# 128-column zero matmuls, a first weight piece of 384 columns on two queues, and two units moved by one place

## The chip, the cores and the metric

The kernel runs on one core of a Trainium2 chip. Its five engines work from streams of their own and meet through semaphores: TensorE (PE in the profile; its weight loads are listed as PEld), VectorE (DVE), ScalarE (ACT), GpSimd (POOL) and SyncE (SP), which here only issues DMA transfers. ScalarE issues a few transfers too. The metric is the device time of one execution in microseconds (us). The profile also gives the span, from the first to the last instruction of the program.

## The reference

The input `x` is 2048 x 512, bfloat16. Its rows are normalized, and the sum of three terms comes out: `x` itself, a spectral filter of the normalized rows, and a gated feed-forward block on them.

```python
def _A_ref(x, w_r, w_i):
    X = jnp.fft.rfft2(x.astype(jnp.float32), axes=(-2, -1))
    X = X * (w_r + 1j * w_i)
    return jnp.fft.irfft2(X, s=(S, D), axes=(-2, -1)).astype(jnp.bfloat16)

def _B_ref(x, w_gate, w_up, w_down):
    g = jnp.einsum("bsd,df->bsf", x, w_gate)
    u = jnp.einsum("bsd,df->bsf", x, w_up)
    return jnp.einsum("bsf,fd->bsd", _gelu(g) * u, w_down)

xn = _layernorm(x, axis=-1)
return x + _A_ref(xn, A_w_r, A_w_i) + _B_ref(xn, B_w_gate, B_w_up, B_w_down)
```

There are 2048 rows, 512 columns and 1792 features between `w_gate`/`w_up` and `w_down`.

## The kernel before

The 2048 rows are 16 tiles of 128 rows; four tiles make a block of 512 rows. The 1792 features are 14 chunks (`fc`) of 128.

**Normalization** (`ln_stats`, `ln_rstd`, `ln_apply`): VectorE takes mean and variance of a tile (L401, L402). The reciprocal root comes from ScalarE for tiles 0 and 1 (L407) and from GpSimd for all later ones (L416, L417). VectorE applies it (L424). TensorE then transposes the tile (L442, four 128 x 128 pieces a tile, against a unit matrix), and VectorE and ScalarE copy the transposes from the accumulation banks into `xnT` (L449, L451).

**Feed-forward**: `geglu_unit(b, fc)` makes one chunk for one block: four matmuls with `wg_sb` and four with `wu_sb` (L499), the gelu on ScalarE (L511), the product on VectorE into `hT` (L519). The first six chunks of block 0 are done in two halves of 256 rows, so that they can begin when tiles 0 and 1 are there. `down_unit(b, jj)` makes one output tile: 14 matmuls of `hT` with `wd_sb` (L547; the last tile in two halves of 14), and the sum into `x_sb` on VectorE (L553).

**Spectral branch**: GpSimd folds the halves of `xnT` (L463, L464), `unit_d` and `unit_A` transform along columns and rows (L571, L587), the result goes through memory (`shuffle`) into another order, `unit_B` and `unit_c` finish the transform, multiply by the filter and go back (L618 to L645), 64 small transfers reorder again (L650), `unit_e` (L665, copied by ScalarE at L670) and `unit_fin` (L685 to L697) come back to rows and columns and add to `x_sb`.

**Order.** Each engine's stream is the order in which the program records its operations; `emit` puts a semaphore wait before an operation where it depends on another engine. An engine never passes an operation that waits. The order on TensorE is written out by hand from L703 on: the zeros, the normalization of tiles 0 and 1, their transposes, the twelve half chunks with the transposes of tiles 2 and 3 between (after the half chunk `fc` 3), and then the spectral units with *fillers* between them. `filler(n)` takes the next n units from one list of all remaining feed-forward units (`geglu_unit` and `down_unit` of blocks 0 to 3 in a fixed order), so that TensorE has work while a spectral unit waits for its copies. `spare` is the number of fillers spread over the 18 steps of `unit_B` and `unit_c`, worked out so that four are left over for the end.

**Zeros.** `warm_up` (L473 to L483) has TensorE multiply zeros, 18 times with 512 columns, from a memset of `hT[1]`; the results are not used. The memset is the third operation on VectorE's stream.

**Transfers.** SP issues nearly all loads in one order, ScalarE the unit matrix and weight piece 0. `WPIECES` cuts the columns of `w_gate` and `w_up` into four pieces, 256, 512, 512 and 512 wide; each piece is two transfers under one semaphore, and a chunk's first matmul waits for both transfers of each piece that its 128 columns touch. So piece 0 serves chunks 0 and 1, piece 1 chunks 2 to 5, piece 2 chunks 6 to 9, piece 3 the rest. The order before: on ScalarE the unit matrix, `wg` and `wu` of piece 0; on SP x tiles 0 to 3 (one each), piece 1, x tiles 4 to 7, piece 2, x tiles 8 to 15, piece 3, constants, `w_down`.

Of the kernel before, what the change touches and what calls it, by code (L numbers as in the profile page):

```python
# [16 lines left out]
FF = 1792  # L17
P = 128
# [3 lines left out]
NFC = 14  # L22
NGG = 3
NX1 = 4
NWARM = 18
LN_EPS = 1e-5


# [131 lines left out]
class _Sched:  # L160
# [14 lines left out]
    def total(self, stream):  # L175
        return (stream, self.stream_cnt[stream])
# [59 lines left out]
def bass_parallel_sum__spectral_gfnet__glu_gated_geglu__prompt_kernel(  # L236
# [15 lines left out]
    xv = A_x.rearrange("b (p j) d -> p (b j) d", j=NJ)  # L252
# [3 lines left out]
    sch = _Sched()  # L256

    with ExitStack() as es:

        def sb(name, shape, dt=BF16):  # L260
            return es.enter_context(nc.sbuf_tensor(name, shape, dt))

        x_sb = sb("x_sb", [P, NJ, D])
        xnT = sb("xnT", [P, NDC, S])
        wg_sb = sb("wg_sb", [P, NDC, FF])
        wu_sb = sb("wu_sb", [P, NDC, FF])
        wd_sb = sb("wd_sb", [P, NFC, D])
        hT = [sb("hT%d" % i, [P, NFC, 512]) for i in range(2)]
# [45 lines left out]
        def bank_of(slot):  # L314
            return ps[:, slot * 512:(slot + 1) * 512]
# [25 lines left out]
        def load(stream, dst, src, eng="sp"):  # L341
            sch.op(eng, lambda e: e.dma_start(dst, src), stream=stream)
            return total(stream)


        ev_id = load("ident", small[:, 0:P], c_small.ap()[:, 0:P], eng="act")
        ev_x = {}
        for j in range(4):
            ev_x[j] = load("x%d" % j, x_sb[:, j, :], xv[:, j, :])

        WPIECES = ((0, 256), (256, 768), (768, 1280), (1280, FF))
        ev_w = {}
        spec = {}

        def load_w(i, eng="sp"):
            a, b = WPIECES[i]
            for dst, src in ((wg_sb, B_w_gate), (wu_sb, B_w_up)):
                load("w%d" % i, dst[:, :, a:b], src[:, a:b].rearrange("(r p) f -> p r f", p=P), eng=eng)
            ev_w[i] = total("w%d" % i)

        def load_xc(m):
            ev = load("xc%d" % m, x_sb[:, 4 * m:4 * m + 4, :], xv[:, 4 * m:4 * m + 4, :])
            for j in range(4 * m, 4 * m + 4):
                ev_x[j] = ev

        load_w(0, eng="act")
        load_w(1)
        load_xc(1)
        load_w(2)
        load_xc(2)  # L370
        load_xc(3)
# [21 lines left out]
            spec["eg"] = total("eg")  # L393


        ev_eps = sch.op("pool", lambda e: e.memset(eps_t[:], LN_EPS))
        ev_half = sch.op("pool", lambda e: e.memset(half_t[:], -0.5))
        ev_ag = {}
# [61 lines left out]
        def folds(m, after=()):  # L460
            sl = slice(m * 512, (m + 1) * 512)
            deps = [ev_xnT[4 * m], ev_xnT[4 * m + 3]] + list(after)
            a = sch.op("pool", lambda e: e.tensor_tensor(fold[:, 0:2, sl], xnT[:, 0:2, sl], xnT[:, 2:4, sl], ALU.add), deps=deps)  # L463
            b = sch.op("pool", lambda e: e.tensor_tensor(fold[:, 2:4, sl], xnT[:, 0:2, sl], xnT[:, 2:4, sl], ALU.subtract), deps=deps)  # L464
            ev_fold[m] = [a, b]
# [4 lines left out]
        hT_readers = [[], []]  # L470
        ev_h_block = {}

        def warm_up():  # L473

            ev = sch.op("dve", lambda e: e.memset(hT[1][:, 0, :], 0.0))

            def f(e):
                ins = None
                for i in range(NWARM):
                    ins = e.matmul(bank_of(7), hT[1][:, 0, 0:P], hT[1][:, 0, :], start=True, stop=True)  # L480
                return ins

            hT_readers[1].append(sch.op("pe", f, deps=[ev]))  # L483

        def geglu_unit(b, fc, a=0, w=512, ring=None):

            k = geg["k"]
            geg["k"] = k + 1
            s2 = k % NGG
            hb = b % 2  # L490
            ring = ring or ring_gu
            evw = [ev_w[i] for i, (lo, hi) in enumerate(WPIECES) if lo < (fc + 1) * P and fc * P < hi]
            evx = [ev_xnT[4 * b + i] for i in range(a // P, (a + w) // P)]
            gslot, gdeps = ring.alloc(1)

            def mm(e, wsb, slot, dcs=range(NDC)):
                ins = None
                for dc in dcs:
                    ins = e.matmul(gu_bank(slot)[:, 0:w], wsb[:, dc, fc * P:(fc + 1) * P], xnT[:, dc, b * 512 + a:b * 512 + a + w],  # L499
                                   start=(dc == 0), stop=(dc == NDC - 1))  # L500
                return ins

            if b == 0 and fc == 0 and a == 0:
                for dc in range(NDC):
                    ev_gm = sch.op("pe", lambda e, dc=dc: mm(e, wg_sb, gslot, (dc,)), deps=evw + [x[dc] for x in evx] + gdeps)
            else:
                ev_gm = sch.op("pe", lambda e: mm(e, wg_sb, gslot), deps=evw + evx + gdeps)
            uslot, udeps = ring.alloc(1)
            ev_um = sch.op("pe", lambda e: mm(e, wu_sb, uslot), deps=udeps)
            gg = gg_sb[s2][:, 0:w]  # L510
            ev_gg = sch.op("act", lambda e: e.activation(gg, gu_bank(gslot)[:, 0:w], ACT.Gelu_apprx_tanh),  # L511
                           deps=[ev_gm] + gg_readers[s2])
            gg_readers[s2] = []
            ring.add_reader(gslot, ev_gg)
            hdeps = []
            if fc == 0 and a == 0:
                hdeps = list(hT_readers[hb])
                hT_readers[hb] = []
            ev_h = sch.op("dve", lambda e: e.tensor_tensor(hT[hb][:, fc, a:a + w], gu_bank(uslot)[:, 0:w], gg, ALU.mult),  # L519
                          deps=[ev_um, ev_gg] + hdeps)  # L520
            ring.add_reader(uslot, ev_h)
            gg_readers[s2].append(ev_h)
            ev_h_block.setdefault(b, []).append(ev_h)
# [9 lines left out]
        def down_unit(b, jj):  # L533
            hb = b % 2
            j = 4 * b + jj

            ring, bank = (ring_gu if b == 3 else ring_dn), bank_of
            parts = 2 if j == NJ - 1 else 1
            w = D // parts
            for h in range(parts):  # L540
                slot, bdeps = ring.alloc(1)
                cs = slice(h * w, h * w + w)

                def f_dn(e, slot=slot, cs=cs):
                    ins = None
                    for fc in range(NFC):
                        ins = e.matmul(bank(slot)[:, 0:w], hT[hb][:, fc, jj * P:(jj + 1) * P], wd_sb[:, fc, cs],  # L547
                                       start=(fc == 0), stop=(fc == NFC - 1))
                    return ins

                ev_dn = sch.op("pe", f_dn, deps=[ev_wd] + list(ev_h_block[b]) + bdeps)
                hT_readers[hb].append(ev_dn)
                ev_a = sch.op("dve", lambda e, slot=slot, cs=cs: e.tensor_tensor(x_sb[:, j, cs], bank(slot)[:, 0:w], x_sb[:, j, cs], ALU.add),  # L553
                              deps=[ev_dn, ev_xn[j]] + ev_acc.get(j, [])[:1])
                ring.add_reader(slot, ev_a)
                finished(j, ev_a, cs, h == 0)
# [102 lines left out]
        def unit_e(j):  # L659
            slot, bdeps = ring_sp.alloc(1)  # L660

            def f_e(e):
                ins = None
                for ci in range(4):
                    ins = e.matmul(sp_bank(slot)[:, ci * P:(ci + 1) * P], V[:, j, V0[ci]:V0[ci] + HD - 1:2], EM[:, j, :], start=True, stop=True)  # L665
                return ins

            ev_p = sch.op("pe", f_e, deps=[spec["perm2_0"], spec["perm2_1"], spec["eg"]] + bdeps)
            src = sp_bank(slot).rearrange("p (ci q) -> p ci q", ci=4)
            ev_ZT[j] = sch.op("act", lambda e: e.activation(ZT[:, :, j, :], src, ACT.Copy), deps=[ev_p] + [spec["dr%d" % q] for q in range(2)])  # L670
            ring_sp.add_reader(slot, ev_ZT[j])
# [29 lines left out]


        warm_up()  # L703
        NHALF = 6
        ln_stats(0)
# [31 lines left out]
        todo = {"left": len(fillers)}  # L737

        def filler(n=1):
            for _ in range(n):  # L740
                u = next(fill, None)
                if u is None:
                    return
                todo["left"] -= 1
                if u[0] == "g":
                    geglu_unit(u[1], u[2])
                else:
                    down_unit(u[1], u[2])
# [2 lines left out]
        for j in range(4, 8):  # L751
            ln_apply(j)
        folds(0, [ev_xn[7]])
        filler()
        transposes(4, 8, ring_tr)
        folds(1)
        filler()
        for m in range(2, NDC + 2):
            for i in range(4):
                j = 4 * (m - 2) + i  # L760
# [25 lines left out]
        load_eg()  # L786
        filler(5)

        spare = todo["left"] - 18 - 2 - 17 - 4
        for u in range(18):  # L790
            if u >= 2:
                unit_c(u - 2)
# [2 lines left out]
            filler(1 + (u + 1) * spare // 18 - u * spare // 18)  # L795
        filler(2)
        for j in range(NJ + 1):
            filler()
            if j < NJ:
                unit_e(j)  # L800
            if j >= 1:
                unit_fin(j - 1)
# [52 lines left out]
```

## Time and profile before

| | us |
|---|---|
| median of three runs | 194.21 (194.02 to 194.59) |
| the profiled execution | 194.54 |
| its span | 192.7 |
| TensorE busy | 188.0 (98% of the span) |
| VectorE, ScalarE, GpSimd busy | 95.1, 90.5, 40.2 |
| first matmul of chunk 0 starts | 8.96 |
| last down units start (L547) | 178.02 |

The chain of work that ended last lies on TensorE for 96% of the span: 49% on L499, 25% on L547, 3.6% on the zeros of L480. The DMA engines are nearly full from 2 to 26 us, when the weights and `x` are loaded. How to read the rows of the timeline in what follows: start and busy time in us, engine, line of the kernel, operation, out<-in, shape, how many were merged into the row, and in brackets the idle time of the engine before it and what ended that. A matmul's row lasts until its results are out, so rows of consecutive matmuls overlap; the pace is read from starts.

### The profile page before, as it was taken

To read this page: it belongs to the slowest core of one execution; us is meant where nothing else is said; L and a number is where in the kernel's file an instruction comes from. 1 tells how busy PE (TensorE), PEld (TensorE's weight loads), DVE (VectorE), ACT (ScalarE), POOL (GpSimd) and SP (SyncE) were. 2 spreads that over 40 slices of the span, in tenths; PEclk is the share of its full clock that TensorE was granted. 3 is DMA by queue.
4 is the path that set the end of the run, shared out by engine and by line. 5 is a ranking of instruction groups with operands and counts; after the bars stand their busy time and mean duration, and the time that the engine had idled before them with its cause. 6 is when DMAs were issued, how large, how long until landed. Compare 5 with 4: busy or idle time off the path is not lost.

```text
span 192.7 us, 3034 instructions
## 1 busy us (share of the span) xinstructions
PE 188.0 (98%) x1120; PEld 104.4 (54%) x1120; DVE 95.1 (49%) x201; ACT 90.5 (47%) x168; POOL 40.2 (21%) x38
## 2 busy tenths in 40 slices
PE   7999999999999999999999999999999999999994
PEld 2488455556554544455555555544555555554453
DVE  4478866966122222276455544524354545456221
ACT  2544346877465562156565464614363634465000
POOL 0010299090800000000000000000224424444200
DMA  5999950999993915801112112210011011010011
GB/s 149 353 374 371 372 174 27 184 198 245 198 179 109 301 66 153 258 0 34 48 49 57 42 50 53 52 44 18 0 58 54 27 54 56 29 54 0 20 38 54
DMA packets 25438, 22.20 MB, mean 115 GB/s; under 512 B 1616, under 2 KB 24656, under 8 KB 25296
## 3 DMA queue, kind: packets, MB, share of 16 engines
q1 hardware_dynamic: 24224, 21.45, 40.9%
q10 hardware_dynamic: 1200, 0.56, 1.0%
q8 instruction: 9, 0.15, 0.3%
q14 instruction: 5, 0.04, 0.1%
HBM read 15.71 MB, written 4.19 MB: 103 GB/s over the span
## 4 chain that ended last, share of the span: by engine, by line
PE 96%; DVE 2%; issue 0%
PE ps L499 49%; PE ps L547 25%; PE ps L571 4%; PE ps L480 4%; PE ps L685 3%; PE ps L665 2%; PE ps L618 2%; PE ps L640 2%; PE ps L639 2%; PE ps L442 2%; PE ps L587 2%; DVE hT L519 1%; DVE bufA L424 1%; DVE x_sb L553 0%; DVE xnT L449 0%
## 5 line engine op out<-in xcount | busy, mean ns | idle before, releaser
L499 PE MATMUL ps<-xnT,wg_sb 128*128 128x512 bf16 (+1 forms) x248 | 58.6, 358 | 0.1
L499 PE MATMUL ps<-xnT,wu_sb 128*128 128x512 bf16 (+1 forms) x248 | 58.5, 358 | 0.0
L519 DVE TENSOR_TENSOR hT<-ps,gg 128x512 bf16<-128x512 f32 (+1 forms) x62 | 39.3, 637 | 31.8 <-PE ps L499 30.3
L547 PE MATMUL ps<-wd_sb,hT 128*128 128x512 bf16 (+1 forms) x238 | 50.5, 366 | 0.3 <-DVE hT L519 0.3
L511 ACT ACTIVATE gg<-ps 128x512 bf16<-128x512 f32 (+1 forms) x62 | 34.5, 556 | 23.8 <-PE ps L499 23.2
L697 POOL TENSOR_TENSOR x_sb<-x_sb,bufC 128x512 bf16<-128x512 bf16 x16 | 18.4, 1152 | 108.8 <-DVE bufC L692 108.8
L499 PEld LDWEIGHTS ps<-xnT,wu_sb 128*128 128x128 bf16 x248 | 24.3, 98 | 24.1
L547 PEld LDWEIGHTS ps<-wd_sb,hT 128*128 128x128 bf16 x238 | 23.2, 98 | 23.8 <-DVE hT L519 0.6
L499 PEld LDWEIGHTS ps<-xnT,wg_sb 128*128 128x128 bf16 x248 | 23.9, 98 | 16.8 <-issue 0.3
L553 DVE TENSOR_TENSOR x_sb<-ps,x_sb 128x512 bf16<-128x512 f32 (+1 forms) x17 | 11.2, 660 | 32.1 <-PE ps L547 32.1
L579 ACT ACTIVATE X<-ps 128x512 bf16<-128x512 f32 x16 | 11.9, 746 | 14.7 <-PE ps L571 14.7
L645 ACT ACTIVATE Vp<-ps 128x514 bf16<-128x514 f32 x16 | 9.6, 600 | 18.9 <-PE ps L640 9.5
L670 ACT ACTIVATE bufA<-ps 128x512 bf16<-128x512 f32 x16 | 9.6, 597 | 17.1 <-PE ps L665 17.1
L626 DVE TENSOR_TENSOR M<-Xc,wr_sb 128x514 bf16<-128x514 bf16 x16 | 6.9, 429 | 14.5 <-ACT Xc L623 14.5
L401 DVE BATCH_NORM_STATS2 st<-x_sb 128x6 f32<-128x512 bf16 x16 | 10.8, 675 | 1.7 <-DMA x_sb<-in_A_x_dram 1.7
L623 ACT ACTIVATE Xc<-ps 128x514 bf16<-128x514 f32 x16 | 9.5, 595 | 4.0 <-PE ps L618 4.0
L463 POOL TENSOR_TENSOR bufB<-xnT 128x1024 bf16<-128x1024 bf16 x4 | 8.5, 2124 | 11.4 <-ACT xnT L451 4.9
L690 DVE TENSOR_TENSOR bufC<-ps,bufC 128x256 bf16<-128x256 f32 x16 | 6.8, 425 | 6.7 <-ACT bufC L689 6.7
L685 PE MATMUL ps<-fa,bufA 128*128 128x256 bf16 x64 | 9.6, 273 | 0.0
L571 PE MATMUL ps<-fa,bufB 128*128 128x256 bf16 x64 | 9.6, 272 | 0.0
L591 ACT ACTIVATE bufA<-ps 128x512 bf16<-128x512 f32 x16 | 9.3, 584 | 0.5 <-PE ps L587 0.5
L464 POOL TENSOR_TENSOR bufB<-xnT 128x1024 bf16<-128x1024 bf16 x4 | 8.5, 2126 | 0.0
(39 smaller groups left out, 123.9 us busy)
## 6 DMA issues: line engine op xcount, KB each, us to landing
stage_p<-bufA SPq DMA_DIRECT2D x16, 128.0 KB, 5.2
bufC<-stage_p SPq DMA_DIRECT2D x4, 512.0 KB, 5.1
bufB<-Vp SPq DMA_DIRECT2D x64, 32.0 KB
out_dram<-x_sb SPq DMA_DIRECT2D x15, 128.0 KB, 1.8
wd_sb<-in_B_w_down_dram SPq DMA_DIRECT2D x1, 1792.0 KB, 14.2
wr_sb<-in_A_w_r_dram SPq DMA_DIRECT2D x6, 257.0 KB, 5.8
wi_sb<-in_A_w_i_dram SPq DMA_DIRECT2D x6, 257.0 KB, 8.2
wg_sb<-in_B_w_gate_dram SPq DMA_DIRECT2D x3, 512.0 KB, 8.8
```

The source lines that it names most:

```text
L401: ev = sch.op("dve", lambda e: e.bn_stats(st[:, j, :], x_sb[:, j, :]), deps=[ev_x[j]])
L499: ins = e.matmul(gu_bank(slot)[:, 0:w], wsb[:, dc, fc * P:(fc + 1) * P], xnT[:, dc, b * 512 + a:b * 512 + a + w], start=(dc == 0), stop=(d ...
L511: ev_gg = sch.op("act", lambda e: e.activation(gg, gu_bank(gslot)[:, 0:w], ACT.Gelu_apprx_tanh), deps=[ev_gm] + gg_readers[s2])
L519: ev_h = sch.op("dve", lambda e: e.tensor_tensor(hT[hb][:, fc, a:a + w], gu_bank(uslot)[:, 0:w], gg, ALU.mult), deps=[ev_um, ev_gg] + hdeps)
L547: ins = e.matmul(bank(slot)[:, 0:w], hT[hb][:, fc, jj * P:(jj + 1) * P], wd_sb[:, fc, cs], start=(fc == 0), stop=(fc == NFC - 1))
L553: ev_a = sch.op("dve", lambda e, slot=slot, cs=cs: e.tensor_tensor(x_sb[:, j, cs], bank(slot)[:, 0:w], x_sb[:, j, cs], ALU.add), deps=[ev_ ...
L571: ins = e.matmul(bank, fold[:, r, j * P:(j + 1) * P], FD[:, r, :], start=(r % 2 == 0), stop=(r % 2 == 1))
L579: ev_X1[j] = sch.op("act", lambda e: e.activation(dst, src, ACT.Copy), deps=[ev_p, X1_readers[j % NX1]])
L645: ev_v = sch.op("act", lambda e: e.activation(Vp[s2][:], sp_pair(slot), ACT.Copy), deps=[ev_p] + Vp_readers[s2])
L670: ev_ZT[j] = sch.op("act", lambda e: e.activation(ZT[:, :, j, :], src, ACT.Copy), deps=[ev_p] + [spec["dr%d" % q] for q in range(2)])
L685: ins = e.matmul(bank[:, h:h + HD], ZT[:, ci, j, :], G[:, ci, :], start=(ci < 2), stop=(ci >= 2))
L697: ev_o = sch.op("pool", lambda e: e.tensor_tensor(x_sb[:, j, :], x_sb[:, j, :], rS[s2], ALU.add), deps=[a, b, ev_xn[j]] + ev_acc.get(j, []))
```

## The change

Four edits:

1. The run of zeros is 46 matmuls of 128 columns instead of 18 of 512. Its memset covers 128 columns instead of 512 and becomes VectorE's first operation.
2. The weight pieces are 384, 512, 384 and 512 columns wide. Piece 0 serves chunks 0 to 2, piece 1 chunks 3 to 6, piece 2 chunks 7 to 9. Of piece 0, ScalarE issues only `wu`; `wg` is issued by SP, between x tiles 1 and 2.
3. Before the transposes of tiles 4 to 7 stand two fillers after `folds(0)` instead of one, and the filler after `folds(1)` is gone: on TensorE chunk 8 of block 0 comes before these transposes instead of after them.
4. In the last loop the filler ahead of the last `unit_fin` is gone; `spare` is one larger, so one filler more runs in the loop of `unit_B` and `unit_c`. On TensorE all fillers of the last loop move up by one place: `unit_e(15)`, `unit_fin(14)` and `unit_fin(15)` now follow the last chunk of block 3 with nothing between them.

```diff
-NWARM = 18
+NWARM = 46
...
-        ev_x = {}
-        for j in range(4):
-            ev_x[j] = load("x%d" % j, x_sb[:, j, :], xv[:, j, :])
-
-        WPIECES = ((0, 256), (256, 768), (768, 1280), (1280, FF))
+        WPIECES = ((0, 384), (384, 896), (896, 1280), (1280, FF))
...
-        def load_w(i, eng="sp"):
+        def load_w(i, which=(0, 1), eng="sp"):
             a, b = WPIECES[i]
-            for dst, src in ((wg_sb, B_w_gate), (wu_sb, B_w_up)):
+            for q in which:
+                dst, src = ((wg_sb, B_w_gate), (wu_sb, B_w_up))[q]
                 load("w%d" % i, dst[:, :, a:b], src[:, a:b].rearrange("(r p) f -> p r f", p=P), eng=eng)
             ev_w[i] = total("w%d" % i)
...
-        load_w(0, eng="act")
+        ev_x = {}
+        load_w(0, (1,), eng="act")
+        for j in range(4):
+            ev_x[j] = load("x%d" % j, x_sb[:, j, :], xv[:, j, :])
+            if j == 1:
+                load_w(0, (0,))
         load_w(1)
...
+        ev_zero = sch.op("dve", lambda e: e.memset(hT[1][:, 0, 0:P], 0.0))
         ev_eps = sch.op("pool", lambda e: e.memset(eps_t[:], LN_EPS))
...
         def warm_up():
-            ev = sch.op("dve", lambda e: e.memset(hT[1][:, 0, :], 0.0))
-
             def f(e):
                 ins = None
                 for i in range(NWARM):
-                    ins = e.matmul(bank_of(7), hT[1][:, 0, 0:P], hT[1][:, 0, :], start=True, stop=True)
+                    ins = e.matmul(bank_of(7)[:, 0:P], hT[1][:, 0, 0:P], hT[1][:, 0, 0:P], start=True, stop=True)
                 return ins
-            hT_readers[1].append(sch.op("pe", f, deps=[ev]))
+            hT_readers[1].append(sch.op("pe", f, deps=[ev_zero]))
...
         folds(0, [ev_xn[7]])
-        filler()
+        filler(2)
         transposes(4, 8, ring_tr)
         folds(1)
-        filler()
...
-        spare = todo["left"] - 18 - 2 - 17 - 4
+        spare = todo["left"] - 18 - 2 - 16 - 4
...
         for j in range(NJ + 1):
-            filler()
             if j < NJ:
+                filler()
                 unit_e(j)
             if j >= 1:
                 unit_fin(j - 1)
```

## The prediction

> **What bounds the kernel now.** I read the head of the page first, then who TensorE waited for, then the timeline of the places where it waited.
>
> ```profile
> span 192.7 us, 3034 instructions
> PE 188.0 (98%) x1120; PEld 104.4 (54%) x1120; DVE 95.1 (49%) x201; ACT 90.5 (47%) x168; POOL 40.2 (21%) x38
> ```
>
> TensorE (PE) is busy for 98% of the span, so only work taken from it, or idle time in it, can be won. Its own waits are three:
>
> ```profile
> PE ps L480 <- DVE hT L475: 1.4, 1, 1.4
> PE ps L442 <- DVE bufA L424: 0.3, 1, 0.3
> PE ps L547 <- DVE hT L519: 0.3, 1, 0.3
> ```
>
> The first is the start, the second (at 24 us) the transposes of tiles 4 to 7, the third (at 178 us) the last block's down projection. "Busy" hides a fourth loss, the zeros. The timeline of the first 16 us (start, busy time, engine, line) shows it:
>
> ```profile
> 1.43 6.94 PE L480 MATMUL ps<-hT 128*128 128x512 bf16 x18 [1.43 <-DVE hT L475]
> 5.37 0.73 DVE L424 TENSOR_SCALAR bufA<-x_sb,ag,rstd 128x512 bf16<-128x512 bf16 x2
> 6.53 0.15 PEld L480 LDWEIGHTS ps<-hT 128*128 128x128 bf16 x1 [0.28 <-issue]
> 6.96 0.15 PEld L480 LDWEIGHTS ps<-hT 128*128 128x128 bf16 x1 [0.28 <-issue]
> 7.34 0.53 PEld L480 LDWEIGHTS ps<-hT 128*128 128x128 bf16 x3 [0.24 <-issue]
> 8.21 0.61 PE L442 MATMUL ps<-small,bufA 128*128 128x128 bf16 x8
> 8.96 0.67 PE L499 MATMUL ps<-xnT,wg_sb 128*128 128x256 bf16 x4
> 10.78 0.60 PE L499 MATMUL ps<-xnT,wg_sb 128*128 128x256 bf16 x4
> 11.65 0.60 PE L499 MATMUL ps<-xnT,wg_sb 128*128 128x256 bf16 x4
> 12.61 0.62 PE L442 MATMUL ps<-small,bufA 128*128 128x128 bf16 x8
> ```
>
> The first two normalized tiles are ready at 5.37 + 0.73 = 6.10, but the transposes that read them stand behind the zeros and start at 8.21: 2.1 us lost. The weight loads give the pace: 0.43 us from one zero matmul to the next up to 6.96, then 0.215 (8.21 less 7.34 is four of them). Thus the array runs at half pace until about 7.3, 5.9 us after the first zero; the granted-clock column says 1.00 all the while, so it doesn't show this. The rows at 10.78, 11.65 and 12.61 are feature chunks fc 2 and fc 3 of block 0 and the transposes of tiles 2 and 3.
>
> How much of the 2.1 us can be had is set by the weights. Before, fc 2 is the first to need piece 1. The issues of the two transfers of `wu` that matter (last number: us from issue to landing; issued at 1.68 and 3.06):
>
> ```profile
> wu_sb<-in_B_w_up_dram ACTq DMA_DIRECT2D x1, 256.0 KB, 5.3
> wu_sb<-in_B_w_up_dram SPq DMA_DIRECT2D x1, 512.0 KB, 7.1
> ```
>
> Piece 0 is in at 7.0 and piece 1 at 10.15, only 0.6 us before fc 2 starts.
>
> **The change, part by part.**
>
> *Zeros.* 18 x 512 columns become 46 x 128. At the shut clock 128 columns take a quarter of 0.427, 0.107 us, so 46 take 4.9 us. The memset now comes first on VectorE and is smaller (the 32-column one took 0.09, the 256-column one 0.27), so the zeros start at about 1.07 instead of 1.43 and end at 5.98, just before 6.10. The upper bound per zero is the 0.151 us of a weight load in this stretch: the end is then near 7.6, as the clock opens at 7.3. I take 0.107: the transposes, also 128 columns and a load each, go at the pace of their columns (16 in 1.07), with 0.098 us loads overlapped.
>
> *The clock.* Transposes start at 6.15 and, shut, take 8 x 0.107 to 7.0. Before, the fourth matmul of the first chain (the last that waits for a copy) started 1.14 us after the first transpose; the slower transposes add 8 x 0.051, so it starts at 7.7. From there to fc 3 are 1 + 4 + 8 + 8 = 21 matmuls of 256 columns at 0.109 us: 2.3 us with the clock open, twice that shut. If it opens at time c, fc 3 can start at 0.5c + 6.14. From the row, 5.9 us after the first zero is c = 7.0, provided that the short break at 6 us and the transposes don't undo it; fc 3 could then start at 10.0.
>
> *The first pieces.* Piece 0 grows by 128 columns of two matrices, 256 KB, ahead of piece 1, which now serves fc 3 to 6. The packet records give 27 ns for 512 B and 46 ns for 1024 B, so I estimate 36.5 ns for the new 768 B. 1024 packets on 16 engines take 2.34 us instead of 1.73: piece 1 lands 0.6 later, at 10.75. Bounds: 0 (the DMA share was 0.75 between 3 and 4 us, which could absorb it) and 262 KB at the lowest rate of a full stretch, 213 GB/s: 1.2 us. I take 0.6, from the packets themselves. So fc 3 starts at 10.8, not 10.0: **piece 1 becomes the bound**, if c is below 9.3. fc 3 runs 0.87 us, and the transposes of tiles 2 and 3 start at 11.67 instead of 12.61. Their tiles are ready by then: statistics to apply took 8.95 to 12.56 before, and should start near 7.35 now, when tiles 2 and 3 have landed behind `wg`'s piece (two x transfers moved past one on SP's queue; they landed at 5.7 and 6.8, I estimate 6.9 and 7.4). Piece 0 itself completes with less queued ahead of it than the 1056 KB of before, by about 7.0, where it is needed; being late by up to 0.8 would cost nothing, since fc 3 waits anyway. ScalarE issues one transfer less, and its table load starts 0.5 earlier, hidden. Piece 2 shrinks, is needed a chunk later, and landed 5 us before need. **Gain 0.94 us.**
>
> *The filler before the transposes.* fc 8 moves ahead of the transposes of tiles 4 to 7 and covers the wait for VectorE at 24 us:
>
> ```profile
> 24.02 1.07 PE L442 MATMUL ps<-small,bufA 128*128 128x128 bf16 x16 [0.35 <-DVE bufA L424]
> 24.11 2.12 POOL L463 TENSOR_TENSOR bufB<-xnT 128x1024 bf16<-128x1024 bf16 x1 [2.08 <-DVE bufA L424]
> 26.19 2.12 POOL L464 TENSOR_TENSOR bufB<-xnT 128x1024 bf16<-128x1024 bf16 x1
> 28.38 0.34 PEld L571 LDWEIGHTS ps<-fa,bufB 128*128 128x128 bf16 x4 [0.34 <-issue]
> ```
>
> fc 7's matmuls end at 23.5, so 0.5 us is idle. But the first unit of the spectral branch (L571) waits for GpSimd's two folds, which end at 28.31, and it came at 28.38. Its chain (tile 7 normalized, then 4.2 us of folds) doesn't move against VectorE, so TensorE would only arrive 0.5 earlier and wait there. Gain 0; ends 0 and 0.5. The second folds start at 28.27 when GpSimd is free, and their input comes at about 27.4 now: still hidden.
>
> *The last filler.* The end of the spectral branch:
>
> ```profile
> 177.07 0.60 PE L685 MATMUL ps<-fa,bufA 128*128 128x256 bf16 x4
> 177.27 0.69 DVE L519 TENSOR_TENSOR hT<-ps,gg 128x512 bf16<-128x512 f32 x1 [0.51 <-PE ps L499]
> 178.02 1.25 PE L547 MATMUL ps<-wd_sb,hT 128*128 128x512 bf16 x5 [0.35 <-DVE hT L519]
> ```
>
> The last chunk's matmuls end at 177.07; one unit of 0.43 covers the 0.95 us until its result is ready, and 0.52 is idle. Now three units follow the last chunk: e(15) of 0.22, fin(14) and fin(15). That chunk ends at 177.07 - 0.66 = 176.41, its result comes at 177.36, but fin(15) waits for ScalarE's copy of e(15): 0.42 from e(15)'s start, then 0.60, so 177.48. It runs to 177.92, against 178.02. **Gain 0.1** (0 to 0.5): one wait takes the other's place. The unit that moved to before the first e unit runs where TensorE never waited; the 64 shuffle transfers get 1.7 us more cover, and output transfers on SP stay off the path.
>
> Sum: 0.94 + 0 + 0.10 = 1.04. The profiled execution took 194.54 (span 192.7, 1.84 around it), 0.33 above the median of 194.21, so 194.54 - 1.04 = **193.5**, 0.37% below the median. With piece 1 at 10.4 to 11.0 it is 193.15 to 193.75.
>
> [...]
>
> **Rivals.** A measurement tells about 0.3% (0.58 us) from no change.
>
> 1. *The clock opens late* (slower). If the break undoes what the zeros did and 5.9 us of work are needed anew, c is 6.15 + 5.9 = 12.05, or 7.7 + 5.9 = 13.6 from the fourth matmul. By 0.5c + 6.14 the head is then 0.52 to 1.29 later than 11.65: 194.54 + 0.52 - 0.1 = 194.95 to 195.75; I take 195.3. It is slower than the profiled run from c = 11.2. For it: the zeros before needed all of 5.9 us. Against: the break is under 0.2 us. Chance 0.16.
> 2. *Piece 1 later, or the clock in between.* With 1.2 us for the 256 KB fc 3 starts at 11.4 and the gain is 0.3; c = 10.2 gives fc 3 at 11.25 and 0.4; zeros of 0.151 us give fc 3 at 11.1 and 0.5. With 0.1 from the end: 193.9 to 194.15, I take 194.05, "same". Chance 0.24.
> 3. *The larger piece is hidden.* Piece 1 lands as before, fc 3 starts at 10.2 and the transposes wait for their tiles until 11.05: gain 1.55 + 0.1, or the folds turn out quicker and 0.5 comes from there: 192.9. Chance 0.08.
>
> The forecast has 0.52. **Numbers.** Below 193.63 lie about 0.8 of the forecast's chance, all of rival 3 and a little of rival 2: faster 0.52, same 0.32, slower 0.16. The range 192.9 to 195.0 leaves out half of rival 3 and most of rival 1.
>
> **What would show it.** Zeros 0.107 us apart ending near 6.0; the weight loads of the first g chain 0.2 us apart until the clock opens, by 9.3; a wait of TensorE for `wu_sb` before fc 3 near 10.8; no wait before the 16 transposes, but a new one before the first L571 unit; a wait for ScalarE's copy before the last fin. It is wrong if the pace stays halved beyond 11 us, if piece 1 comes after 11.2, or if the folds don't hold the first L571 unit.

## The result, and the profile after

The changed kernel takes **193.28 us** (median of 12 runs, 193.04 to 193.94) against 194.21 (12 runs): a ratio of 0.9959, 95% interval 0.9947 to 0.9972. The forecast was 193.5, in a range from 192.9 to 195.0. The profiled execution took 193.59 with a span of 191.8; it stands 0.31 above its median, as that of before stood 0.33 above its own, so the two profiles can be laid side by side: their times are 0.95 us apart.

TensorE's waits after (who waited for whom, us in total, times, longest):

```profile
PE ps L481 <- DVE hT L398: 1.0, 1, 1.0
PE ps L445 <- DVE bufA L427: 0.7, 1, 0.7
PE ps L500 <- DMA wu_sb<-in_B_w_up_dram: 0.5, 1, 0.5
PE ps L572 <- issue: 0.4, 1, 0.4
PE ps L686 <- ACT bufA L671: 0.3, 1, 0.3
```

The two later waits of the list of before, at 24 and at 178 us, are gone, and four others stand in their place: for the first tiles (L445, at 6.67), for weight piece 1 (L500), before the first spectral unit (L572) and before the last fin (L686). The head, in the timeline after:

```profile
0.97 5.02 PE L481 MATMUL ps<-hT 128*128 128x128 bf16 x46 [0.97 <-DVE hT L398]
5.79 0.73 DVE L427 TENSOR_SCALAR bufA<-x_sb,ag,rstd 128x512 bf16<-128x512 bf16 x2
6.67 0.61 PE L445 MATMUL ps<-small,bufA 128*128 128x128 bf16 x8 [0.68 <-DVE bufA L427]
7.42 0.67 PE L500 MATMUL ps<-xnT,wg_sb 128*128 128x256 bf16 x4
9.23 0.60 PE L500 MATMUL ps<-xnT,wg_sb 128*128 128x256 bf16 x4
10.82 0.61 PE L500 MATMUL ps<-xnT,wg_sb 128*128 128x256 bf16 x4 [0.55 <-DMA wu_sb<-in_B_w_up_dram]
11.70 0.61 PE L445 MATMUL ps<-small,bufA 128*128 128x128 bf16 x8
```

The transposes of tiles 0 and 1 start 1.54 us earlier (6.67 against 8.21), chunk 2 starts 1.55 earlier (9.23 against 10.78), and then TensorE waits for `wu` of piece 1: chunk 3 starts at 10.82 against 11.65, the transposes of tiles 2 and 3 at 11.70 against 12.61. Of 1.54 us won by the zeros, 0.91 are left. The two moved units, in the timeline after:

```profile
24.32 1.06 PE L445 MATMUL ps<-small,bufA 128*128 128x128 bf16 x16
25.27 2.12 POOL L467 TENSOR_TENSOR bufB<-xnT 128x1024 bf16<-128x1024 bf16 x1
26.07 1.03 PE L500 MATMUL ps<-xnT,wu_sb 128*128 128x512 bf16 x4
27.50 0.60 PE L572 MATMUL ps<-fa,bufB 128*128 128x256 bf16 x4 [0.40 <-issue]
...
175.78 0.60 PE L686 MATMUL ps<-fa,bufA 128*128 128x256 bf16 x4
176.63 0.61 PE L686 MATMUL ps<-fa,bufA 128*128 128x256 bf16 x4 [0.25 <-ACT bufA L671]
```

The 16 transposes no longer wait, but the first spectral unit starts at 27.50 against 28.41: still 0.91 earlier, no more; the second fold ends at 25.27 + 2.12 = 27.39 and holds it.

The idle times in brackets count from a modelled end; read from starts, the waits are longer. Consecutive matmuls of 512 columns start 0.216 us apart and of 256 columns 0.109 apart, so after the four from 26.07 the next could start at 26.94, and 0.56 is lost before 27.50; after the four from 175.78 it could start at 176.22, and 0.41 is lost before 176.63. In the profile of before the same reading gives 0.51 before the transposes at 24.02 and 0.51 before the last down units at 178.02. So the moved chunk changes 0.51 into 0.56 and the last filler 0.51 into 0.41; together they gain 0.05. That is all that the change gains behind the head: from the transposes of tiles 2 and 3 to the end of the span it is 180.13 us before and 180.09 after.

### The profile page after: what moved, and what is told of

Read it like the earlier page. It is cut to its first block, busy times and chain, and to the rows that moved or that the text cites. A ratio compares the mean times of both kernels' runs of the same rounds, so it can differ in the third digit from the quotient of the medians.

```text
span 191.8 us, 3072 instructions
## 1 busy us (share of the span) xinstructions
PE 185.4 (97%) x1129; PEld 106.7 (56%) x1148; DVE 94.5 (49%) x201; ACT 90.0 (47%) x168; POOL 40.2 (21%) x38
## 4 chain that ended last, share of the span: by engine, by line
PE 86%; DMA 7%; SPq 3%; issue 2%; ACT 1%; DVE 0%; ACTq 0%
PE ps L500 46%; PE ps L548 23%; DMA wu_sb<-in_B_w_up_dram 4%; PE ps L572 4%; PE ps L686 4%; DMA bufB<-Vp 3%; PE ps L666 2%; PE ps L445 2%; PE ps L588 2%; PE ps L640 1%; PE ps L641 1%; SPq L342 1%; PE ps L619 1%; SPq L651 1%; ACT Xc L624 1%
## 5 line engine op out<-in xcount | busy, mean ns | idle before, releaser
L500 PE MATMUL ps<-xnT,wg_sb 128*128 128x512 bf16 (+1 forms) x241 | 57.4, 358 | 1.1 <-DMA wu_sb<-in_B_w_up_dram 0.5
L500 PE MATMUL ps<-xnT,wu_sb 128*128 128x512 bf16 (+1 forms) x245 | 58.0, 358 | 0.2
L548 PE MATMUL ps<-wd_sb,hT 128*128 128x512 bf16 (+1 forms) x230 | 49.8, 366 | 0.4
L500 PEld LDWEIGHTS ps<-xnT,wu_sb 128*128 128x128 bf16 x248 | 24.3, 98 | 24.1
L500 PEld LDWEIGHTS ps<-xnT,wg_sb 128*128 128x128 bf16 x248 | 23.9, 98 | 17.8 <-DMA wu_sb<-in_B_w_up_dram 0.8
L554 DVE TENSOR_TENSOR x_sb<-ps,x_sb 128x512 bf16<-128x512 f32 (+1 forms) x17 | 11.2, 659 | 30.6 <-PE ps L548 30.6
L404 DVE BATCH_NORM_STATS2 st<-x_sb 128x6 f32<-128x512 bf16 x16 | 10.8, 675 | 2.3 <-DMA x_sb<-in_A_x_dram 2.3
L466 POOL TENSOR_TENSOR bufB<-xnT 128x1024 bf16<-128x1024 bf16 x4 | 8.5, 2123 | 11.4 <-ACT xnT L454 4.9
L572 PE MATMUL ps<-fa,bufB 128*128 128x256 bf16 x64 | 9.6, 272 | 0.4 <-issue 0.4
L686 PE MATMUL ps<-fa,bufA 128*128 128x256 bf16 x64 | 9.6, 273 | 0.3 <-ACT bufA L671 0.3
L572 PEld LDWEIGHTS ps<-fa,bufB 128*128 128x128 bf16 x64 | 6.2, 98 | 4.8 <-issue 0.9
```

Source lines behind the costliest of these rows:

```text
L404: ev = sch.op("dve", lambda e: e.bn_stats(st[:, j, :], x_sb[:, j, :]), deps=[ev_x[j]])
L572: ins = e.matmul(bank, fold[:, r, j * P:(j + 1) * P], FD[:, r, :], start=(r % 2 == 0), stop=(r % 2 == 1))
L686: ins = e.matmul(bank[:, h:h + HD], ZT[:, ci, j, :], G[:, ci, :], start=(ci < 2), stop=(ci >= 2))
```

## The experiments

The theory to be tested: the short zeros give TensorE a head start, weight piece 1 takes part of it back, and the two moved units only exchange one wait for another. The main rival on the other side is the clock (that is, whether TensorE runs at half or at full pace), if the break before the transposes undoes the zeros. All ratios are against runs of the kernel before on the same chip.

**Each part alone.** First the zeros, on the kernel before:

```diff
-NWARM = 18
+NWARM = 46
...
+        ev_zero = sch.op("dve", lambda e: e.memset(hT[1][:, 0, 0:P], 0.0))
...
-                    ins = e.matmul(bank_of(7), hT[1][:, 0, 0:P], hT[1][:, 0, :], start=True, stop=True)
+                    ins = e.matmul(bank_of(7)[:, 0:P], hT[1][:, 0, 0:P], hT[1][:, 0, 0:P], start=True, stop=True)
```

> The kernel before with the 46 short zeros alone (and their earlier memset); pieces and fillers as before. Theory (head start, then the weight piece binds): the transposes start near 6.5 instead of 8.21, but chunk 2 needs piece 1, which lands at 10.15 here, so it starts near 10.2 instead of 10.78, with a wait for wu_sb in front: 0.5 us gained, 193.7. Rival (all of the gain is that of the zeros, and the pieces count for nothing): the time of the whole change, 193.3.

Measured: 193.95 against 194.11, ratio 0.9993 (0.9977 to 1.0008). The median gains 0.16 where 0.4 was expected (193.7), though the interval just reaches that far; the rival of 193.3 falls. The timeline of TensorE in this run shows what the head start runs into:

```profile
6.30 0.86 PE L443 MATMUL ps<-small,bufA 128*128 128x128 bf16 x8 [0.24 <-DVE bufA L425]
7.15 0.77 PE L498 MATMUL ps<-xnT,wg_sb 128*128 128x256 bf16 x4
10.07 0.61 PE L498 MATMUL ps<-xnT,wg_sb 128*128 128x256 bf16 x4 [0.84 <-DMA wu_sb<-in_B_w_up_dram]
11.83 0.61 PE L443 MATMUL ps<-small,bufA 128*128 128x128 bf16 x8
```

The transposes start 1.9 us earlier than in the first profile of before, and chunk 2 then waits 0.84 for piece 1, which it needs in this cut of the weights. With the old pieces, the head start runs into piece 1 one chunk earlier. The expectation was worked out from a late profile: in the two runs further down that leave zeros and pieces as before, full pace came sooner, the transposes start at 7.35 and 7.42, and chunk 2 at 10.21 and 10.06, when its piece 1 lands (3.1 + 7.1 and 3.1 + 7.0). There the short zeros have next to nothing to give: the transposes of tiles 2 and 3 start at 11.96 and 11.82 in those two, and at 11.83 here.

The pieces and queues alone:

```diff
-        WPIECES = ((0, 256), (256, 768), (768, 1280), (1280, FF))
+        WPIECES = ((0, 384), (384, 896), (896, 1280), (1280, FF))
...
-        load_w(0, eng="act")
+        load_w(0, (1,), eng="act")
+        for j in range(4):
+            ev_x[j] = load("x%d" % j, x_sb[:, j, :], xv[:, j, :])
+            if j == 1:
+                load_w(0, (0,))
```

> The kernel before with the new pieces and queues alone; 18 zeros of 512 columns. Theory: the transposes stay behind the zeros until about 8.2, chunk 3 starts at 11.65 as before, and piece 1 lands at 10.75, in time: no change, 194.2. Rival (the pieces help by themselves, or the larger piece 0 hurts): chunk 0 waits for piece 0, or chunk 3 for piece 1, and the time moves by 0.3 us or more.

Measured: 193.82 against 194.11, ratio 0.9987 (0.9970 to 1.0004), no difference that this interval shows; it doesn't exclude the rival's 0.3 us either. Its profile does not look like that of before: the 18 zeros reach full pace at 4.1 us instead of 7.3, the transposes of tiles 0 and 1 start at 6.65 and those of tiles 2 and 3 at 11.21. Chunk 3 starts at 10.33, when piece 1 lands (3.6 + 6.7), so even with the old zeros an early full pace brings TensorE to piece 1. So the same 18 zeros reach full pace at different times, 2.7 us after the first zero here and 5.9 in the profile of before; more on this below.

The filler before the transposes alone, and the last filler alone:

```diff
         folds(0, [ev_xn[7]])
-        filler()
+        filler(2)
         transposes(4, 8, ring_tr)
         folds(1)
-        filler()
```

> The kernel before with chunk 8 moved ahead of the transposes of tiles 4 to 7 alone. Theory: the wait of TensorE before these transposes goes (0.5 us), and the same comes back before the first unit of the spectral branch, which waits for the folds that end at 28.3: no change, 194.2. Rival (the wait is a real loss): 0.5 us gained, 193.7.

```diff
-        spare = todo["left"] - 18 - 2 - 17 - 4
+        spare = todo["left"] - 18 - 2 - 16 - 4
...
-            filler()
             if j < NJ:
+                filler()
                 unit_e(j)
```

> The kernel before with the last loop's fillers one place earlier alone. Theory: the 0.5 us before the last down units goes, and a wait for the copy of e(15) before fin(15) comes, near 0.4: gain 0.1, 194.1. Rival (the full wait is won): gain 0.5, 193.7.

Measured: 194.06 (1.0000, 0.9985 to 1.0015) and 194.14 (1.0000, 0.9984 to 1.0015), both against 194.11. TensorE's waits with the first of the two edits:

```profile
PE ps L480 <- DVE hT L475: 1.4, 1, 1.4
PE ps L571 <- issue: 0.4, 1, 0.4
PE ps L547 <- DVE hT L519: 0.3, 1, 0.3
```

The wait of L442 is gone and a wait of 0.4 before L571 has come, as the theory says. With the second edit the wait of L547 is gone and this row has come, in the timeline of TensorE:

```profile
177.20 0.61 PE L685 MATMUL ps<-fa,bufA 128*128 128x256 bf16 x4 [0.25 <-ACT bufA L670]
```

(This profile has one wait more, 0.4 us for ScalarE's `Vp` at 123 us; the profile of the changed kernel, with the same edit, doesn't have it.) Both rivals of 0.5 us fall. The medians of the four parts alone add up to 0.2%, the whole change has 0.41%. That the zeros and the pieces need each other is argued, from the wait in the run with the zeros alone and its place one chunk earlier; the intervals of the parts are too wide to prove it by their sum, and no run has these two parts together without the moved units.

**The clock.** Fewer zeros in the changed kernel:

```diff
-NWARM = 46
+NWARM = 12
```

> The changed kernel with 12 zeros instead of 46: they end near 2.3 us, and TensorE is then without work until its first tiles are ready near 6.5. Theory (the clock opens only after several us of work just before): half pace from the transposes on, for 4.8 to 5.9 us, so until 11 to 12.5; chunk 3 starts at about 0.5c + 6.3, 11.8 to 12.5, instead of 10.82: 194.2 to 194.9. Rival (the pace opens by itself, by time from the start): the same as the changed kernel, 193.3.

```diff
-NWARM = 46
+NWARM = 30
```

> The changed kernel with 30 zeros: they end near 4.2 us, a break of 2.3 us before the transposes. Theory (a break undoes the zeros): as with 12 zeros, 194.2 to 194.9. Rival (a break of 2.3 us is too short to matter, what counts is work within some us): the clock opens by 9.3, piece 1 still binds, 193.3.

Measured: 194.33 against 194.16 with 12 zeros (1.0021, 0.9998 to 1.0044; single runs from 193.73 to 196.13), and 194.13 with 30 (1.0011, 0.9990 to 1.0031; 193.37 to 195.36). Both medians have lost the gain of the change, as expected (30 zeros came out just under the 194.2 to 194.9), and their runs spread by 2 us and more, where those of the changed kernel spread by 0.9. The timeline of TensorE with 12 zeros:

```profile
6.93 1.01 PE L445 MATMUL ps<-small,bufA 128*128 128x128 bf16 x8 [4.50 <-DVE bufA L427]
7.78 1.03 PE L500 MATMUL ps<-xnT,wg_sb 128*128 128x256 bf16 x4
8.61 1.06 PE L500 MATMUL ps<-xnT,wu_sb 128*128 128x256 bf16 x4
9.46 1.06 PE L500 MATMUL ps<-xnT,wg_sb 128*128 128x256 bf16 x4
...
12.02 0.69 PE L500 MATMUL ps<-xnT,wu_sb 128*128 128x256 bf16 x4
12.55 0.60 PE L500 MATMUL ps<-xnT,wg_sb 128*128 128x256 bf16 x4
13.43 0.61 PE L445 MATMUL ps<-small,bufA 128*128 128x128 bf16 x8
```

Four matmuls of 256 columns take 0.85 us from start to start until 12.0, and 0.44 from 12.55 on: half pace until 12.2, for 5.3 us from the first transpose on. Chunk 3 starts at 12.55, no wait for piece 1 is left, and this execution took 195.24. With 30 zeros (a break of 2.1 us) full pace comes at 9.9, 3.5 us after the first transpose, and that execution took 193.91. The rival that the pace comes by time from the start falls. That a break undoes the zeros is not shown by these two runs, because their zeros never reached full pace: they are 0.107 us apart to the last one. What the runs show is that 12 or 30 zeros do not carry over a break of 2 us and more; the price, as in the forecast, is about 0.5 us for each us of half pace that chunks 0 to 2 can't hide behind piece 1.

More zeros, and a larger piece 0:

```diff
-NWARM = 46
+NWARM = 58
```

> The changed kernel with 58 zeros: at 0.107 us until the clock opens near 5.7 and 0.056 after, they end near 6.6 to 7.1, up to 0.5 us after the tiles are ready. Theory (piece 1 binds, with 0.7 us of slack on TensorE before it): chunk 3 still starts when piece 1 is in, 193.3, same as the changed kernel. Rival (the end of the zeros sets the time): up to 0.5 us later, 193.8.

```diff
-        WPIECES = ((0, 384), (384, 896), (896, 1280), (1280, FF))
+        WPIECES = ((0, 512), (512, 896), (896, 1280), (1280, FF))
```

> The changed kernel with pieces of 512, 384, 384 and 512 columns, so that chunk 3 needs piece 0. Theory (the wait for piece 1 before chunk 3 costs 0.7 us): piece 0 lands near 7.3 and holds chunk 0 by 0.2 at most, chunks 0 to 3 run without a wait, the transposes of tiles 2 and 3 start when their tiles are ready near 11.3, against 11.70: 0.4 us gained, 192.9. Rival (the loading of all weights binds whatever the cut, or chunk 0 waits for piece 0 as long): 193.3 or more.

Measured with 58 zeros: 193.39 against 194.16, ratio 0.9977 (0.9962 to 0.9992), not to be told from the changed kernel. In its profile the transposes start at 7.08 and the wait for `wu` is gone from the list: TensorE reaches chunk 3 just as piece 1 lands at 10.6. The slack before piece 1 is real, and 0.4 us of it was spent for nothing. Here it was not the zeros that spent it: full pace came at 5.1, they ended at 6.2, and the transposes waited 0.7 for their tiles, whose x landed late, at 3.9. In the last run below the zeros are what the transposes wait for.

Measured with 512 columns: 193.42 against 194.16, ratio 0.9973 (0.9950 to 0.9996): nothing gained, the expectation of 192.9 falls. The timeline of TensorE says why:

```profile
7.83 0.61 PE L500 MATMUL ps<-xnT,wg_sb 128*128 128x256 bf16 x4 [0.93 <-DMA wg_sb<-in_B_w_gate_dram]
11.80 0.62 PE L445 MATMUL ps<-small,bufA 128*128 128x128 bf16 x8 [0.31 <-DVE bufA L427]
```

Chunk 0 now waits for piece 0 (landed at 7.8, not 7.3), and the transposes of tiles 2 and 3 wait for their tiles, whose x landed at 8.1 and 8.6 behind the larger piece. Another cut only chooses which transfer is waited for.

**Taking the new waits away.** The two waits that the moved units left behind, in the changed kernel:

```diff
         transposes(4, 8, ring_tr)
         folds(1)
+        filler()
```

> The changed kernel with one filler more between the second folds and the first spectral unit (two chunks there instead of one). Theory (the first spectral unit waits 0.4 to 0.5 us for the folds): the wait is covered, 0.4 us gained, 192.9. Rival (the idle time moves on to a later unit, or the filler is missed at its old place): 193.3.

```diff
-            if j < NJ:
+            if j < NJ - 1:
                 filler()
+            if j < NJ:
                 unit_e(j)
+            if j == NJ - 1:
+                filler()
```

> The changed kernel with e(15) before the last chunk instead of after it. Theory (fin(15) waits 0.25 to 0.4 us for ScalarE's copy of e(15)): the copy is ready by then, the last chunk's result is ready just as fin(15) ends, and 0.3 us is gained, 193.0. Rival (the wait for the last chunk's result takes its place whole): 193.3.

Measured: 192.67 against 194.30 with the filler before the first spectral unit (0.9919, 0.9896 to 0.9941), and 193.12 with e(15) before the last chunk (0.9948, 0.9930 to 0.9967). The first lies clear of the changed kernel's interval, the second doesn't. In the first run's list of waits L572 is gone, in the second's L686, and no other has come in their place. From the transposes of tiles 2 and 3 to the end of the span it is 180.1 us in the changed kernel (191.8 less 11.7), 179.5 in the first run and 179.7 in the second: 0.6 and 0.4 less, as long as the two waits are when they are read from starts (0.56 and 0.41). By the times alone the second rival, 193.3, is not excluded; the list and this stretch speak against it.

All three edits together:

> The changed kernel with all three: a filler more before the first spectral unit, e(15) before the last chunk, and pieces of 512, 384, 384 and 512. Theory (three separate waits on TensorE's path): the gains add, 0.4 + 0.3 + 0.4, 192.2. Rival (one takes the place of another): 192.9 or more.

Measured: 192.51 against 194.30 (0.9922, 0.9896 to 0.9948), from 192.31 to 193.76. The 192.2 of three gains falls. By the times alone this run can't be told from the one with the first edit; the profile shows that the two gains add: from the transposes of tiles 2 and 3 to the end it is 179.1 us, 1.0 less than in the changed kernel. The pieces add no third. The profiled execution is the one of 193.76, and its timeline of TensorE holds a surprise:

```profile
6.35 0.61 PE L445 MATMUL ps<-small,bufA 128*128 128x128 bf16 x8 [1.05 <-DVE bufA L427]
7.67 1.00 PE L500 MATMUL ps<-xnT,wg_sb 128*128 128x256 bf16 x4 [0.71 <-DMA wg_sb<-in_B_w_gate_dram]
9.32 1.06 PE L500 MATMUL ps<-xnT,wg_sb 128*128 128x256 bf16 x4
11.53 0.60 PE L500 MATMUL ps<-xnT,wu_sb 128*128 128x256 bf16 x4
```

The transposes run at full pace (0.61 for eight), the chunks after the wait at half pace again (0.85 from start to start), and full pace returns at 11.2. This time the granted clock shows it too, in tenths (9 is 90% or more), one digit for 4.8 us:

```profile
PEclk9889999999999999999999999999999999999999
```

Taken in windows of 0.02 us it falls to 0.50 at 7.74 and is back at 1.00 at 11.16. The zeros had reached full pace at 4.33 and so ended at 5.1, and two breaks of 1.05 and 0.71 us followed. Breaks of this length don't always do it: in the run with the pieces of 512 columns alone full pace came at 4.1, the breaks were 1.12 and 0.93, and the chunks after them run at full pace.

The last run leaves the pieces as the change has them, takes both edits against the new waits, and lengthens the zeros so that an early full pace leaves a shorter break:

```diff
-NWARM = 46
+NWARM = 58
...
         folds(1)
+        filler()
...
+            if j == NJ - 1:
+                filler()
```

> The changed kernel with the filler before the first spectral unit, e(15) before the last chunk, and 58 zeros instead of 46; pieces as in the change. Theory: the two waits of 0.4 and 0.25 us go and add up, and longer zeros leave a shorter break before the transposes, so that the half pace does not come back in some runs: 192.5, about 0.7 below the changed kernel, with a narrower spread. Rival (one of the two gains only, or the longer zeros cost what they cover): 192.9 or more.

Measured: **192.48** against 194.14, ratio 0.9918 (0.9902 to 0.9934), from 192.26 to 192.87. It beats both kernels; its interval lies below that of the change. From the transposes of tiles 2 and 3 to the end it is again 179.1 us. What the longer zeros are worth is not shown: this interval also covers the run with the first edit alone (0.9919), the narrow spread stands on six runs, and the twelve of the changed kernel with 58 zeros spread by 1.4, more than those with 46. That they cost nothing is: in this profile the tiles are ready at 6.28, the zeros end at 6.57, and TensorE still waits for piece 1 after that. After the start, only one wait of TensorE is left in the list:

```profile
PE ps L481 <- DVE hT L398: 1.0, 1, 1.0
PE ps L500 <- DMA wu_sb<-in_B_w_up_dram: 0.3, 1, 0.3
```

## Why the prediction was right, point by point

- **The zeros.** 0.107 us apart, as worked out; they started at 0.97 (forecast 1.07) and the last began at 5.75. Right.
- **The first tiles** were ready at 6.52, not 6.10: the first x tile landed 2.8 us after its issue instead of 2.4. It cost nothing, since the wait for piece 1 was 0.55 long (0.71 from starts). The forecast took the landing of one profile as fixed; over all the profiles here the tile is in between 3.1 and 3.9 us.
- **The clock** opened after the last zero began at half pace, at 5.75, and before the transposes, which run at full pace from 6.67: below the 9.3 from which it would have decided. That case was right, but the step that gave c = 7.0, "5.9 us after the first zero", was not: over the profiles of 18, 46 and 58 zeros full pace came between 2.7 and 5.9 us after the first zero. What sets the moment, no run shows. The profile of before was a late one. The same 18 zeros reach full pace at 4.1 in the run with the pieces alone and at 7.3 there, so profiles with the zeros and pieces of before differ from one another in the head: the transposes of tiles 2 and 3 start at 12.61 in the first profile, and at 11.96 and 11.82 in the two runs that leave zeros and pieces alone. In the eight profiles that have, behind these transposes, the waits of before or of the change and no others (before; the change; the zeros alone; the moved chunk alone; 12, 30 and 58 zeros; 512 columns), the time less the start of these transposes is 181.8 to 182.0, so it is the head that makes the times of these kernels differ. By that a median run of before has this start near 12.3, and one of the changed kernel near 11.4 (estimates: 194.21 and 193.28 less 181.9). Laying one profile of after against one of before gave the right sum by luck: both stood 0.3 above their medians.
- **Piece 1 becomes the bound.** Forecast landing 10.75, measured 3.6 + 7.2 = 10.8; chunk 3 forecast at 10.8, measured 10.82; the gain up to the transposes of tiles 2 and 3 forecast as 0.94, measured 0.91. The estimate of 36.5 ns for a packet of 768 B stood: the packet records after have a median of 36. That the landing came within 0.05 is partly luck, since with the same pieces it came at 10.3 in the run of the pieces alone and at 10.4 in the last run.
- **The filler before the transposes**: forecast 0, measured -0.05 in the change (0.51 lost before, 0.56 after) and 1.0000 alone, with the new wait at the place named. The wait is TensorE's for the folds, as forecast.
- **The last filler**: forecast 0.10, measured 0.10 (0.51 lost before, 0.41 after), with the wait for ScalarE's copy. The terms of the forecast, 0.42 and 0.60 from the start of e(15), add up to 177.43 and not to the 177.48 given; from start to start the profile after has 1.07 (175.56 to 176.63), which is the 177.48.
- **The sum** was 1.04; the profiled spans differ by 0.95, which is 0.91 from the head and 0.04 from the two moved units, and the medians by 0.93. The end gave its 0.10, and the moved chunk took half of it back.
- **The rivals.** The late clock (0.16) did not come in the change, but its price is real: with 12 zeros full pace came at 12.2, and chunk 3 at 12.55, where 0.5c + 6.14 gives 12.2 and the later first tiles the rest. What the forecast missed is that a clock that opens *early* lengthens the break: zeros at full pace end sooner (at 5.1 in the run with all three edits, which left a break of 1.05 us), and in that run half pace came back. That piece 1 would land late, or be hidden, fell by the landing at 10.8.

## What to carry to other kernels

A run of filler work is paid for twice, once by its length and once by what it leaves waiting behind it; but its removal is worth only as much as the next late input allows, so look up when the next transfer lands before counting the gain. Moving a unit in front of a wait does nothing when the next unit in line waits for the same chain: count the work between the source of the chain and its last reader, and put the cover there, as the extra filler before the first spectral unit did, for 0.6 us. And parts of a change that show nothing alone may still be worth something together, when one moves the work and the other the input that it needs; run the pair to know.

## What the runs showed of the hardware

- In the profiles here the pace of TensorE's array starts at half (0.107 us for 128 columns, 0.427 for 512) and doubles (0.056 and 0.216) at a time that differs even between runs with the same zeros: 2.7 and 5.9 us after the first zero in two profiles with 18 of them, and within that range in those with 46 and 58. In this first stretch of half pace the granted-clock column says 1.00 (before from 1.40 to 7.30, after from 0.90 to 5.80), so the pace is read from the starts of matmuls.
- It can fall back, and then the column shows it. In the run with all three edits full pace came at 4.33, was lost at 7.74 and came back at 11.16, with the column at 0.50 between the last two. These times are 3.41 and 3.42 us apart. The mean granted clock of that execution is 0.991; three executions with 30 zeros (194.59 to 194.82) and one with the pieces of 512 columns (195.67) have the same mean, and none of them was profiled.
- What makes it fall was not shown either. In that run TensorE was busy for about 38% of the time from 4.33 to 7.74 (zeros until 5.1, eight transposes, the start of chunk 0), worked out from the matmul starts. In the run with 512 columns it was busy for about 37% of the time from full pace at 4.1 to the start of chunk 0 at 7.83, and the pace stayed in that execution.
- In the run with the zeros alone full pace came during the transposes, at 6.9, after a break of 0.4 us between zeros and transposes. Whether transposes bring full pace as zeros do, no run here was made to separate.
